# A gated linear attention with a fast-product MLP: exp(L) stored with adjacent words, single first loads, a LayerNorm step moved, and a new sequence of turns

## The chip, the cores and the metric

The kernel runs on one core of one Trainium2 chip. The metric is the device time of one execution in microseconds (us), the median of several runs. The engines are TensorE (PE; its weight loads are PEld), VectorE (DVE), ScalarE (ACT), GpSimd (POOL) and SyncE (SP), whose queue issues almost all DMAs here. [...]

## The reference

Two blocks follow each other. The first is a recurrent gated linear attention over 4 batches, 8 heads, 768 tokens and heads of 48:

```python
for t in range(S):
    state = alpha[:, :, t, :, None] * state + einsum('bhd,bhe->bhde', k[:, :, t], v[:, :, t])
    y[:, :, t] = einsum('bhd,bhde->bhe', q[:, :, t], state)
```

The second is a feed-forward block on the heads side by side (rows of 384), with the weights given as 64-bit floats:

```python
xn = (x - mean(x)) / sqrt(var(x) + 1e-06) * g_ln
out = x + maximum(xn @ w_ch1, 0.0) @ w_ch2        # 384 -> 1536 -> 384
```

## The kernel before, in words

The 768 tokens are cut into six chunks of 128. `attention(c, b)` treats chunk c of batch b, 24 units in all. With L the running sum of log(alpha) within a chunk (or within each half chunk of 64 tokens from chunk 1 on), k is divided by exp(L) and q multiplied by it, so that attention inside the chunk is a masked product of matrices and the state is carried from half to half.

A unit goes like this. ScalarE takes the logarithm of alpha (L285). TensorE sums it with a triangular matrix into PSUM (`lps`, L288). ScalarE writes exp(L) into the tile `eq` in SBUF (L291) and exp(-L) in place (L292). VectorE forms k·exp(-L) (L294) and q·exp(L) (L296) in the tile `qk`. TensorE transposes both (`tps`, L323), ScalarE or VectorE copies them out (`kT`, and `qT` or `at`; L328 to L333), TensorE multiplies them (`aps`, L340 or L345), and VectorE copies the allowed half into `at` (L353, L356). TensorE forms the update of the state (`ups`, L372), which VectorE adds to the state `st` (L384 in chunk 0, L387 later) and GpSimd multiplies by the gate (L389). TensorE forms the output (`yps`, L399). ScalarE copies it to `x` (L403). LayerNorm follows: statistics on VectorE (L418, L419), the reciprocal deviation on ScalarE (L422, L423), and the last step `xn`, which is one VectorE instruction (L427) in chunks 0 and 1, and from chunk 2 on a small VectorE instruction (L430) and one on ScalarE (L432). TensorE transposes `xn` (`xps`, L439) and ScalarE copies it to `xT` (L441).

The gate is exp(L) of the last token of the half: it lies in one row of `eq` (one partition) and is needed as a column. L301 stores that row to DRAM (`row`), L361 loads it back turned (`gate`). In `eq` the index of the head pair p runs fastest, so each exp writes words four apart, and the gate load reads four adjacent words for each partition.

The MLP works by chunk on all four batches. In chunk 0 it is plain: hidden products (L462, `hidden`), projections (L474, `project`). From chunk 1 on both products use fast schemes with fewer products: 15 for the first layer on sums of weight blocks and of token blocks (L702, `hidden_product`), 20 for the second (L545, `product`). The sums of the weights are formed once, on GpSimd (L655, the turns "S") and VectorE (L505, "W"), those of the inputs per chunk on VectorE (L678, "X"; L532, "N"). Products are combined from PSUM by VectorE and GpSimd (L710 to L745), and ScalarE applies the ReLU (L754, "R").

The weights come as 64-bit floats in twelve pieces of 768 KB (`take_weights`, turns "A" to "L"). Three staging buffers `ws` hold them; VectorE and ScalarE turn each piece into 32-bit floats (L203 to L218). A piece is loaded (L191) when an earlier one has left its buffer.

Everything is written as generators. The string `ORDER` names, one letter per step, which generator goes on: "a" to "x" are the 24 attention units (four letters per chunk), "M" the MLP, "O" the reloading of `x` for the final addition. This string sets the order of every queue:

```python
with tc.manual_schedule():
    for turn in ORDER:
        next(turns[turn], None)
```

Of the kernel before, what the change touches and what calls it, by code (L numbers as in the profile page):

```python
# [9 lines left out]
FP32 = mybir.dt.float32  # L10
# [12 lines left out]


ORDER = (
    "bbBBaddbcccaaaabbdccadabbcbbaaaabdacbbbcccbAcfcaabddddadbeBAbfffeeAgaeeaaccccdbb"
    "chbcaaaaaabbhcdddahfeefAeggghddAddcccbceefffabacefdddbdjcedccfffddDDjgeeeiMMMeeB"
    "iCCDCMMMgCiieeMeejCFMMgggBEEMfjDMfffhhEEfffjigFFfMggggHHeGMMFMGHfhMffgIGMhhgggOO"
    "OOMMMhMggiGJhhSSglMhhjMifHKlIIIMJJhhgiSfSkhMMiiKkeLLKLLhhMMfhheejkMjMeMeJfWeehgg"
    "WMMMFkhhhhhhhggfkMggiWWLgXXOXXXiiiXXSSSSllllmSXXiiiMiMMjMEjjjSSSSSjjMMMMMMMMMMXn"  # L30
    "SSljjjjOMXSMMMjjlMiijWliimWMMlmlklllllmmlMMMMkjjklkMMMMMMkMMmmiikkkkMRRkkMRRWkoM"
    "WWMMMMkknnklMWlljllmnRWRnMmMmjMMoMMMMMMMjjMMMMikiMoRRMMMRMMmmmmmkkkMMMomnnnMMNNo"
    "noWlmpmmRRRMMniWNNNMMMmmmnnnqnnOMMMlnnppNpppNiniMMMMoKMNNlnNMNMoMMoOMMjjNMMNlNMM"
    "NMMMMNMMnkkoooonokoMMMMoooMMkkllpqroXnnXXppMMXXXXMrrqpXXXMMMooXGrppppIpMMqnpMMMp"
    "MMMMMMMMMMMMqqsssRRMMMmmmMRqqMMnpMMMqqrMMMmrtqqqqMMMstsMMMsqqMMMMtMMMMMMqmRpoppM"
    "pRMRRMMMMRRMMRMMRNoooOOOMmmOMMNMqMMrptttsrNNNnMnMMrrMNNNMpMMMMrprrrKvMMrppNNvvMr"
    "rRNNuoJNqnnMMMMMqsqMsMMMMMNNNMMMorvppMMMMooMMssssssMXXsXOMMrMMrOrXXXXtttMMMXXrXX"
    "BssuuMMMMMMMMqMqqqMMMOMMMMMsMMqRMMMMrstCttRssttMMMMMMMMtttMMMMrRRuuvvxOMMMMMMquu"
    "uMMMwMMMMqqvRRRRMMMMMMMMRRMuMMMNNNNMMRRwtutwwwNNMMMNNNtvuuuuMttvttvAMMMMMNNNMMss"
    "ssrrMMMxrxutMMtNMMOMNMMMrMMNNtMMMMMtutxMMsssvvvvrOuuXXXXXXXvuuwMMMMwwwMMXXxXMMMM"  # L40
    "MXMMMMMMMMMMMvMxMMMMMMMMwwwwwvvxxuuuuuDMMvMMMMwMwOMMMMMMMMMxMMMMwRRRMMMxMMMMRRRM"
    "MxxxxxwMMRRRRMNuRvvwNNwwwxMMMvvMuNNNMMMMMMwMMMMMNMNxNNRNNNxxMMOvvMMMMMNMwMMMxxxx"
    "wMMwwxNMMxMMMMxNxvvMMXXMXMXXXXMMXXXMMMMMMMMMMMXMMMMMMMMMMMMMMMMMMMMMMMMMMMMMMMMM"
    "MMMMMMMMMMMMRRMRRRROOORRRRMMMMNNMMMNNRMMNNRMMMMMMNNNNMMMNMMMOMMNNMMMMMMNNMMMNMMM"
    "MMMMMHMM"
)


# [1 line left out]
def kernel(  # L50
# [36 lines left out]
    nc = tc.nc  # L87

    B, S, H, D = q.shape
    DM = H * D  # L90
    DF = w_ch1.shape[1]
    P = 128
    NCB = S // P
    NP = H // 2
# [6 lines left out]
    cpool = ctx.enter_context(tc.tile_pool(name="const", bufs=1))  # L101
# [11 lines left out]
    r = np.arange(P)  # L113
# [5 lines left out]
    def load(c, m, names):  # L119

        bs = range(2 * m, 2 * m + 2)
        rows = slice(c * P, (c + 1) * P)
        for n, src in (("a", alpha), ("k", k), ("q", q)):
            if n in names:
                t = raw.tile([P, 2, 2, NP, D], FP32, name=f"r{n}", tag=f"r{n}")
                nc.sync.dma_start(t.rearrange("t b i p d -> t b (i p d)"),
                                  src[bs.start:bs.stop, rows].rearrange("b t h d -> t b (h d)"))
                raws.update({(n, c, b): t[:, b - bs.start] for b in bs})
        if "v" in names:
            va = raw.tile([P, 2, 2, 2, NP, D], FP32, name="va", tag="va")  # L130
            if c == 0:
                nc.sync.dma_start(va[:, :, 0].rearrange("t b i p d -> t b (i p d)"),
                                  v[bs.start:bs.stop, rows].rearrange("b t h d -> t b (h d)"))
                raws.update({("v", c, b): (None, va[:, b - bs.start]) for b in bs})
                return


            rv = raw.tile([P, 2, NP, D], FP32, name="rv", tag="rv")
            src = v[bs.start:bs.stop, rows].rearrange("b (s t) (i p) d -> i s t b (p d)", s=2, i=2)
            for i in range(2):  # L140
                nc.sync.dma_start(rv[halves[i]].rearrange("t b p d -> t b (p d)"), src[i, i])
                for s in range(2):
                    nc.sync.dma_start(va[halves[1 - i], :, s, i].rearrange("t b p d -> t b (p d)"),
                                      src[i, s])
            for b in bs:
                raws["v", c, b] = rv[:, b - bs.start], va[:, b - bs.start]
# [18 lines left out]
    for m in range(B // 2):  # L165
        load(0, m, "a")
# [54 lines left out]
    def take_weights(i):  # L221
# [13 lines left out]

    more = cpool.tile([P, 4, NJ // 3 * DM // 2], FP32, name="more")
    shared = more.rearrange("p i m -> p (i m)")[:, :4 * NP * P]
    eqs = [cpool.tile([P, 2, 64, NP], FP32, name=f"eq{b}") for b in range(2)]
    eqs += [shared[:, i * NP * P:(i + 1) * NP * P].rearrange(
        "p (b c a) -> p b c a", b=2, c=64) for i in range(2)]  # L240
    qks = [cpool.tile([P, 2, NP, 2, 64], FP32, name=f"qk{b}") for b in range(3)]
    qks.append(shared[:, 2 * NP * P:].rearrange("p (i a b c) -> p i a b c", i=2, b=2, c=64))
    sts = [cpool.tile([R, NP, D], FP32, name=f"st{b}") for b in range(B)]
    for b in range(B):
        nc.vector.memset(eqs[b][:, :, D:], 0.0)
        nc.vector.memset(qks[b].rearrange("p i a b c -> p (i a b) c")[:, :, D:], 0.0)


# [6 lines left out]
    def eq_of(c, b):  # L255
        return eqs[b if c < 2 else b % 2]

    def qk_of(c, b):
        return qks[b if c < 2 else b % 3]
# [12 lines left out]
    def attention(c, b):  # L272


        whole, last = c == 0, c + 1 == NCB
        if whole and b % 2 == 0:
            load(0, b // 2, "kq")
            yield
            load(0, b // 2, "v")
            yield  # L280

        qk = qk_of(c, b).rearrange("t n p i c -> t n i p c")[:, :, :, :, :D]
        eq = eq_of(c, b).rearrange("t i c p -> t i p c")[:, :, :, :D]
        la = work.tile([P, 2, NP, D], FP32, name="la", tag="la")
        nc.scalar.activation(out=la, in_=raws.pop(("a", c, b)), func=AFT.Ln)  # L285
        yield
# [10 lines left out]
        ends = slice(P - 1, P) if whole else slice(HS - 1, P, HS)  # L297
        ne = 1 if whole else 2
        row = dram.tile([2, 2 * 64 * NP], FP32, name="row", tag="row")
        gate = work.tile([P, 2, NP], FP32, name="gate", tag="gate", bufs=B)  # L300
        nc.sync.dma_start(row[:ne], eq_of(c, b)[ends].rearrange("o i c p -> o (i c p)"))  # L301
        yield
        n = c * B + b + 2
        if c < 2 and b % 2:
# [14 lines left out]
        rows = [slice(0, 64), slice(64, R)]  # L319
# [28 lines left out]
        for i in range(2):  # L348
            h = slice(0, P) if whole else halves[1 - i]
# [8 lines left out]
                    mask=mask[h, h].unsqueeze(1).unsqueeze(1).broadcast_to([HS, NP, 2, HS]))  # L358
        yield
        with nc.allow_non_contiguous_dma(reason="two rows to columns"):  # L360
            nc.sync.dma_start(gate[:, :ne], row[:ne].rearrange("o (r p) -> r o p", p=NP))  # L361
        yield
        rv, va = raws.pop(("v", c, b))
        heads = [slice(0, 64), slice(64, R)]
# [58 lines left out]
        nc.scalar.activation(out=rstd[:, :1], in_=rstd[:, :1], func=AFT.Exp, scale=-0.5)  # L423
        yield
        xn = work.tile([P, DM], FP32, name="xn", tag="xn", bufs=2)
        if c < 2:
            nc.vector.tensor_scalar(out=xn, in0=x, scalar1=mv[:, 0:1], scalar2=rstd[:, :1],  # L427
                                    op0=AOP.subtract, op1=AOP.mult)
        else:
            nc.vector.scalar_tensor_tensor(out=rstd[:, 1:], in0=mv[:, 0:1], scalar=-1.0,  # L430
                                           in1=rstd[:, :1], op0=AOP.mult, op1=AOP.mult)
            nc.scalar.activation(out=xn, in_=x, func=AFT.Identity, scale=rstd[:, :1],  # L432
                                 bias=rstd[:, 1:])
# [323 lines left out]
    def mlp():  # L757
        for c in range(NCB):
# [12 lines left out]
            for n in SECOND:  # L771
                yield from product(c, n)

    turns = {chr(ord("a") + n): attention(n // B, n % B) for n in range(NCB * B)}
    turns |= {chr(ord("A") + i): take_weights(i) for i in range(len(pieces))}
    turns |= {"M": mlp(), "S": combine_first(), "W": combine_weights(), "R": relus(),
# [34 lines left out]
```

## Time and profile before

| | us |
|---|---|
| median of 3 runs (lowest, highest) | 482.97 (481.81, 483.08) |
| the profiled execution | 481.5 |
| its span on the core | 479.7 |
| TensorE busy in the span | 454.8 |
| VectorE busy | 366.5 |
| ScalarE busy | 219.8 |
| GpSimd busy | 177.6 |

The mean granted clock of TensorE was 0.989. The busy time of TensorE is modelled at the ends of its pipelined matmuls, so it overstates the work. Lines such as L427 are lines of this kernel; a group in the profile is written as engine, operation, output<-inputs, shapes and count, then busy us and mean ns of one, then the idle time of the engine just before and what ended it. The chain of waits follows the execution back from its last instruction, at each step to what released it.

### The profile page before, as it was taken

The page shows a single profiled execution, that of the slowest core. Times are in us where ns is not written, and L with a number is a line of the kernel's source. Part 1 is how long each engine was busy: PE and PEld are TensorE (multiplying, and loading weights), DVE is VectorE, ACT ScalarE, POOL GpSimd, SP SyncE. Part 2 cuts the span into 40 slices and gives each one's busy share as a digit, 9 for nine tenths or more (in the row PEclk, how much of TensorE's full clock was granted, in tenths as well). Part 3 has the DMA queues.
Part 4 walks back from the last instruction along what each step waited for, and adds up shares of the span by engine and source line. Part 5 has one row for each costly group of instructions (what it writes and reads, how often), then busy time and mean ns, then how long its engine had stood idle before and what let it go on. Part 6 is the DMA issues. An engine that isn't in the chain of part 4 may idle for free.

```text
span 479.7 us, 10173 instructions
## 1 busy us (share of the span) xinstructions
PE 454.8 (95%) x4010; PEld 377.1 (79%) x4010; DVE 366.5 (76%) x687; ACT 219.8 (46%) x463; POOL 177.6 (37%) x199
## 2 busy tenths in 40 slices
PE   6898989997999999999999999999999999998996
PEld 4676454664678889998789898889998899977896
DVE  4798999877758979958978777669767687775683
ACT  4497655534226766345556515555242733213300
POOL 1000040335088571141752242670325450434613
PEclk9899999998999999999999999999999999999999
DMA  8938578233142332222225015022112010120001
GB/s 270 316 89 267 168 248 256 89 83 122 34 129 59 102 108 68 84 67 84 83 86 165 3 50 164 20 84 64 58 40 60 1 51 1 58 91 0 1 10 57
DMA packets 41224, 45.47 MB, mean 95 GB/s; under 512 B 9773, under 2 KB 37293, under 8 KB 41177
## 3 DMA queue, kind: packets, MB, share of 16 engines
q1 hardware_dynamic: 40632, 44.69, 30.0%
q8 instruction: 31, 0.51, 0.4%
q10 hardware_dynamic: 544, 0.13, 0.2%
q14 instruction: 17, 0.13, 0.1%
HBM read 35.28 MB, written 9.53 MB: 93 GB/s over the span
## 4 chain that ended last, share of the span: by engine, by line
PE 54%; DVE 23%; POOL 8%; DMA 5%; ACT 5%; issue 4%; SPq 0%; POOLq 0%; DVEq 0%; ACTq 0%
PE ops L545 20%; PE hps L702 18%; DMA ws<-in_moe_w_ch_dram 5%; PE ops L474 3%; PE aps L345 3%; PE yps L399 2%; PE tps L323 2%; DVE w L205 2%; PE lps L288 2%; DVE at L356 2%; DVE sum L678 2%; DVE qk L296 2%; DVE ws L211 2%; DVE sum L532 2%; PE ups L372 1%
## 5 line engine op out<-in xcount | busy, mean ns | idle before, releaser
L389 POOL TENSOR_TENSOR st<-st,gate 112x192 f32<-112x192 f32 x36 | 27.3, 762 | 129.1 <-DVE st L387 99.8
L702 PE MATMUL hps<-sum,w 128*128 128x256 f32 x240 | 59.1, 381 | 1.1 <-DVE hT L745 1.1
L561 POOL TENSOR_TENSOR ob<-ob,u 128x192 f32<-128x192 f32 x40 | 25.5, 647 | 73.7 <-DVE ob L558 52.0
L702 PEld LDWEIGHTS hps<-sum,w 128*128 128x128 f32 x240 | 44.8, 190 | 8.2 <-DVE hT L745 1.9
L545 PE MATMUL ops<-w,hT 128*128 128x192 f32 x280 | 50.1, 328 | 0.0
L545 PEld LDWEIGHTS ops<-w,hT 128*128 128x128 f32 x280 | 45.6, 190 | 0.7 <-DVE ob L555 0.2
L754 ACT ACTIVATE hT<-hT 128x512 f32<-128x512 f32 x60 | 34.3, 622 | 15.3 <-POOL hT L740 5.1
L379 ACT COPY va<-st 64x192 f32<-64x192 f32 x80 | 27.9, 348 | 27.3 <-POOL st L389 26.5
L356 DVE COPY_PREDICATED at<-consts,aps 64x512 f32<-64x512 int32 x40 | 29.2, 731 | 10.7 <-PE aps L345 9.5
L462 PE MATMUL hps<-xT,w 128*128 128x512 f32 x72 | 33.5, 612 | 0.6 <-ACT x L403 0.6
L474 PE MATMUL ops<-w,hT 128*128 128x384 f32 x96 | 33.3, 500 | 0.0
L399 PEld LDWEIGHTS yps<-va,at 128*64 128x64 f32 (+1 forms) x768 | 24.9, 137 | 10.5 <-issue 5.6
L702 PE MATMUL hps<-xT,w 128*128 128x256 f32 x120 | 31.7, 387 | 1.1 <-DVE hT L734 1.0
L399 PE MATMUL yps<-va,at 128*64 128x48 f32 (+1 forms) x768 | 28.3, 224 | 2.7 <-ACT va L379 2.4
L721 POOL TENSOR_TENSOR hT<-hT,u 128x512 f32<-128x512 f32 x10 | 12.8, 1283 | 48.0 <-DVE u L720 48.0
L545 PE MATMUL ops<-ws,hT 128*128 128x192 f32 x160 | 29.6, 328 | 0.1
L545 PE MATMUL ops<-ws,sum 128*128 128x192 f32 x160 | 29.1, 328 | 0.2 <-DVE ob L558 0.2
L323 PE MATMUL tps<-consts,qk 128*112 128x128 f32 x176 | 26.9, 283 | 1.8 <-DVE qk L294 1.2
L333 ACT COPY at<-tps 64x512 f32<-64x512 f32 (+1 forms) x40 | 23.1, 578 | 11.5 <-PE tps L323 7.5
L474 PEld LDWEIGHTS ops<-w,hT 128*128 128x128 f32 x96 | 18.5, 198 | 11.9 <-issue 0.9
L545 PEld LDWEIGHTS ops<-ws,sum 128*128 128x128 f32 x160 | 26.2, 190 | 0.9 <-DVE ob L558 0.5
L323 PEld LDWEIGHTS tps<-consts,qk 128*112 128x112 f32 x176 | 20.4, 137 | 8.1 <-DVE qk L294 2.1
(154 smaller groups left out, 1051.3 us busy)
## 6 DMA issues: line engine op xcount, KB each, us to landing
ws<-in_moe_w_ch_dram SPq DMA_DIRECT2D x12, 768.0 KB
kept<-x SPq DMA_DIRECT2D x24, 192.0 KB
ob<-kept SPq DMA_DIRECT2D x24, 192.0 KB
va<-in_v_dram SPq DMA_DIRECT2D x40, 96.0 KB
out_dram<-ob SPq DMA_DIRECT2D x19, 192.0 KB
ra<-in_alpha_dram SPq DMA_DIRECT2D x6, 384.0 KB
rk<-in_k_dram SPq DMA_DIRECT2D x6, 384.0 KB
rq<-in_q_dram SPq DMA_DIRECT2D x6, 384.0 KB
```

Of the source, the lines that this page charges most:

```text
L323: nc.tensor.transpose(tps[:, p], qk_of(c, b)[:, i, p].rearrange("p a b -> p (a b)")[:, :R], ident)
L333: nc.scalar.copy(out=at[rows[j], :, j], in_=tv[rows[j]])
L356: nc.vector.copy_predicated(out=at[h, :, i], data=aps[i][h], mask=mask[h, h].unsqueeze(1).unsqueeze(1).broadcast_to([HS, NP, 2, HS]))
L379: nc.scalar.copy(out=to[h, s, i], in_=st[h])
L389: nc.gpsimd.tensor_mul(st, st, by)
L399: nc.tensor.matmul(yps[halves[s], i, p], at[rs, p, i, s], va[rs, 0 if whole else s, i, p], start=True, stop=True)
L462: nc.tensor.matmul(hps, w1[:, f, j * P:(j + 1) * P], xT_of[c][:, f], start=(f == 0), stop=(f == NF - 1))
L474: nc.tensor.matmul(ops_of[b], hT_of[c][:, j, b], w2[:, j], start=(j == 0), stop=(j == NJ - 1))
L545: nc.tensor.matmul(acc, lhs[:, j], rhs[:, j], start=(j == 0), stop=(j == NT - 1))
L561: getattr(nc.gpsimd, f"tensor_{op}")(x, x, y)
L702: nc.tensor.matmul(acc[:, i], w, b, start=True, stop=True)
L754: nc.scalar.activation(out=x, in_=x, func=AFT.Relu)
```

## The change

Four things change. The tile `eq` gets the layout [pair, half, word], so that each exp writes, and each product reads, runs of adjacent words; the row stored to DRAM keeps this order, and the gate load reads single words 128 apart. The alphas of chunk 0 are loaded with one DMA per batch instead of one per two batches. LayerNorm's last step goes to ScalarE from chunk 1 on instead of from chunk 2 on (`whole` is true in chunk 0 only). And `ORDER` is another string with the same letters in the same numbers; only its beginning is shown.

```diff
 ORDER = (
-    "bbBBaddbcccaaaabbdccadabbcbbaaaabdacbbbcccbAcfcaabddddadbeBAbfffeeAgaeeaaccccdbb"
-    "chbcaaaaaabbhcdddahfeefAeggghddAddcccbceefffabacefdddbdjcedccfffddDDjgeeeiMMMeeB"
+    "aBaaabaaabbbbacccadaaaddBbbbdcbbdcceaaaaccbbbbABBfddcabccdddeeceabfgAffaaAccecch"
+    "cbbeggdfgbccacbbbdddbfeedeeddfgaaeaafeeeeCddedcffhafeddcceecOfBeaegbbgfccecdddhg"
...
@@ load @@
-                nc.sync.dma_start(t.rearrange("t b i p d -> t b (i p d)"),
-                                  src[bs.start:bs.stop, rows].rearrange("b t h d -> t b (h d)"))
+                step = 1 if n == "a" and c == 0 else 2
+                for i in range(0, 2, step):
+                    nc.sync.dma_start(
+                        t[:, i:i + step].rearrange("t b i p d -> t b (i p d)"),
+                        src[bs.start + i:bs.start + i + step, rows].rearrange(
+                            "b t h d -> t b (h d)"))
...
-    eqs = [cpool.tile([P, 2, 64, NP], FP32, name=f"eq{b}") for b in range(2)]
+    eqs = [cpool.tile([P, NP, 2, 64], FP32, name=f"eq{b}") for b in range(2)]
     eqs += [shared[:, i * NP * P:(i + 1) * NP * P].rearrange(
-        "p (b c a) -> p b c a", b=2, c=64) for i in range(2)]
+        "p (a b c) -> p a b c", b=2, c=64) for i in range(2)]
...
-        nc.vector.memset(eqs[b][:, :, D:], 0.0)
+        nc.vector.memset(eqs[b].rearrange("p a b c -> p (a b) c")[:, :, D:], 0.0)
...
@@ attention @@
-        eq = eq_of(c, b).rearrange("t i c p -> t i p c")[:, :, :, :D]
+        eq = eq_of(c, b).rearrange("t p i c -> t i p c")[:, :, :, :D]
...
-        nc.sync.dma_start(row[:ne], eq_of(c, b)[ends].rearrange("o i c p -> o (i c p)"))
+        nc.sync.dma_start(row[:ne], eq_of(c, b)[ends].rearrange("o p i c -> o (p i c)"))
...
-            nc.sync.dma_start(gate[:, :ne], row[:ne].rearrange("o (r p) -> r o p", p=NP))
+            nc.sync.dma_start(gate[:, :ne], row[:ne].rearrange("o (p r) -> r o p", p=NP))
...
-        if c < 2:
+        if whole:
             nc.vector.tensor_scalar(out=xn, in0=x, scalar1=mv[:, 0:1], scalar2=rstd[:, :1],
                                     op0=AOP.subtract, op1=AOP.mult)
```

Lines of the changed kernel stand four further down from the alphas' load on.

More of the change, by code (lines that the diff above doesn't have):

```diff
@@ L25 @@
 ORDER = (
-    "bbBBaddbcccaaaabbdccadabbcbbaaaabdacbbbcccbAcfcaabddddadbeBAbfffeeAgaeeaaccccdbb"
-    "chbcaaaaaabbhcdddahfeefAeggghddAddcccbceefffabacefdddbdjcedccfffddDDjgeeeiMMMeeB"
[L28 to L43, printed above, removed]
@@ L44 @@
-    "MMMMMMMMMMMMRRMRRRROOORRRRMMMMNNMMMNNRMMNNRMMMMMMNNNNMMMNMMMOMMNNMMMMMMNNMMMNMMM"
-    "MMMMMHMM"
+    "aBaaabaaabbbbacccadaaaddBbbbdcbbdcceaaaaccbbbbABBfddcabccdddeeceabfgAffaaAccecch"
+    "cbbeggdfgbccacbbbdddbfeedeeddfgaaeaafeeeeCddedcffhafeddcceecOfBeaegbbgfccecdddhg"
+    "gAAfMMfCECfffCCgfMhhiMMMEMMiiEfDjhFkDDiiFFfggMMMhghMMMMffkDGGkEEHHhhGgkFjgjHMijj"
+    "GggMMSMgggggSJhhJjkhhhhHffMMMJfefMMIiiKIiiIIMMOOhhhhhOihhggLLiliiLhKKWeeMMklkllW"
+    "WWIeejjiiliMMMMMSiSSSSSggelfhhhejgMfMhjWgghXXXMXjjjjXSSXXjSXXXiMnjjMMninjMjnjiWl"
@@ new lines @@
+    "llSlnmWiMMMMMMMXSSMMSSMMMMSkMMMjjiiOOkkOWiMMMmMmlllljjjMMMMnMMMMMMMMRjpkkMMGMMMM"
+    "llmMMMWmmWolRRMMMMllllMWnRRnknOiRkkknMMiMMMRMMMMkkkkRMkpRMiimmmmMMjMMMjjHNNmmWmm"
+    "MMMMRRMRNmmNMMmmNNNNMnnnlnnMppMMMpooopnnnMMMMorroqnnnmmNNNroNMMkllkkMMMNNMMMlMMk"
+    "noWkoolMMNNMMkMqMMmlllMppMMkkrXXXXXXXMMMXXoommmooMMMoMMpopoorMrMMppppMppXXMMMMMt"
+    "toqpqtMMMrppmmRMMMMmqMqsMMMRMMRoprMMnnnpqqMMMMooMMMMMMppMpoooMMqMMMMMqqOOOOqqqtM"
+    "MMMMMqqMRRRRRRMMMMsRMMssnoopprmJmtMMMMRNNtNNvrMRoMtqMqrrronrNMssuMMrMBNNMpMvDNMM"
@@ new lines @@
+    "MMNNrNMnnMMrrMMNNMrMppNNMvMMvNMMMMMMMMMAqOXXXXXXrrqqsMMMMsssXXXXXMMMMMMOMKrrMMqt"
+    "ttMMMMMMrssssssMuuMMMMsssMMMMMqqttttMMtqMMRRMRuuutttMMMMMMqsrrrwtvtttqCMMvMMMMMv"
+    "vsuuMMMsMMRRvwstuuvMMMMwssMMMMMvvvvvvwMMwwRuuRuuuqRROORNNMNMRMMNNMMMMMMMNMMttNNN"
+    "MMMMMtrMRtNNNMMMrMMqssMMNNMNNMMMMMtMMMMxxxxMMssMtXXXXXXXXXXxMMvvuuuwwwXMMMMMMMMM"
+    "uuuuxMMMMMMMxMMMMMMRROxMMwvMMMMvxMMMMwvwwwRRMRMMMMwMMxwMMMMMuMMMxxxxuuxMMMMMMMMM"
+    "MRRMMRRRxxMMMOMMOMNNRMNwNNNxNwMMMMMMwwwNNNRxxMMMMxNMMOMMMNNMMMwwvMMvvvxxxMMwMMux"
@@ L46 @@
+    "NNNMMMMuxwxMMwwMvvXXXXXXXMXMMMMMMXXXMMMMMMMMMMMMMMMMMMMMMRRRMMMRLLMMMOKMMMMMMMMM"
+    "MMMMMMMMMMMRRRRMMMMMMMMRRJOOOFMMMMNNNNMRRMMMMMNNNNMMMMMMMNNNMMMMMMNNMMMMMMMNNMMM"
+    "MNMMMMMM"
 )
```

## The prediction

> **What bounds the kernel now.** I read the page first: busy shares, then the span in 40 slices.
>
> ```profile
> PE 454.8 (95%) x4010; PEld 377.1 (79%) x4010; DVE 366.5 (76%) x687; ACT 219.8 (46%) x463; POOL 177.6 (37%) x199
> ...
> PE   6898989997999999999999999999999999998996
> ...
> DVE  4798999877758979958978777669767687775683
> ```
>
> From slice 10 (120 us) on TensorE is full and VectorE is not; before that VectorE is the full one. To see what each stage costs, I add up the work that stands ahead of a step in TensorE's own queue, and subtract the sum from the time at which the step starts: I call this the lag. The sums take the order of the program's instructions and the spacing of matmul records in back-to-back runs (chain of waits: 48 records of L702 in 10.36 us, 128 of L545 in 21.17, 8 of L474 in 2.58; a matmul is two records, a transpose one). Before: first hidden product (L462) 29.6 us of work ahead, starts at 45.8, lag 16.2; first projection (L474) 72.9, 92.9, lag 20.0; fifth projection group 88.6, 108.5, lag 19.9; sixth 92.1, 115.6, lag 23.5; first product of chunk 1 (L702) 113.1, 136.8, lag 23.7; the same line in the last chunk 395.5, 421.4, lag 25.9; near the end 441.3, 470.6, lag 29.3. So 23.7 of the 29.3 us that TensorE loses are lost before 137 us, 3.5 of them between the fifth and the sixth group. The chain of waits, in order of time, shows those:
>
> ```profile
> 110.83 4.02 DVE xn L427
> 114.85 0.04 issue
> 114.89 0.90 PE xps L439 x3
> 115.79 6.21 PE ops L474 x16
> ```
>
> and the timeline shows why a step that takes 0.48 us elsewhere took 4.01:
>
> ```profile
> 110.49 4.12 POOL L655 TENSOR_TENSOR w<-w 128x384 f32<-128x384 f32 x6
> ...
> 110.83 4.01 DVE L427 TENSOR_SCALAR xn<-x,mv,rstd 128x384 f32<-128x384 f32 x1 [1.56 <-ACT rstd L423]
> ```
>
> It ran exactly until GpSimd's row of six ended. From 24 to 107 us the chain is mostly VectorE rounding weights, with DMA waits. VectorE's own lag moves little there: L211 of the second weight piece has 26.8 us ahead and starts at 35.1 (8.3); the last L214 ends with 94.5 done, at 106.8 (12.3).
>
> [...] the exp that writes every fourth word (L291) takes 879 ns, the same exp in place (L292) 606; the product that reads it (L296) takes at least 840, its twin without a stride (L294) 544. [...] In the packet records the 16-byte packets of a gate load start 5.8 ns apart within a burst, far below the loads' 1536-byte packets (median 65 ns each).
>
> ```profile
> L291 ACT ACTIVATE eq<-lps 128x384 f32<-128x384 f32 x20 | 17.6, 879 | 10.4 <-PE hps L702 5.6 <-PE lps L288 4.6
> L292 ACT ACTIVATE lps<-lps 128x384 f32<-128x384 f32 x24 | 14.5, 606 | 0.0
> ...
> L432 ACT ACTIVATE xn<-x,rstd 128x384 f32<-128x384 f32 x16 | 11.3, 707 | 33.7 <-DVE rstd L430 33.7
> ```
>
> ```profile
> L296 DVE TENSOR_TENSOR qk<-rq,eq 128x384 f32<-128x384 f32 x20 | 19.0, 955 | 0.0
> ```
>
> **The change part by part.** *exp(L) with adjacent words.* 24 exps lose 0.27 us of latency each on ScalarE (the next instruction starts 0.65 after such an exp, 0.51 to 0.57 after L292, so occupancy falls less, some 2.5 us in all). 24 products lose 0.28 to 0.30 each (0.84 to about 0.55): 7 us. Only those in VectorE's full stage count: 11 stand ahead of the last weight piece in the new order, 3.2 us.
>
> *The gate load* (L361) now gathers single words: 512 or 1024 packets for 128 or 256, 22,528 instead of 5,632. Lower bound by the bursts: 16 engines, 8 or 16 packets each before, 32 or 64 after, at 5.8 ns: 0.14 or 0.28 us later per load. Upper bound: the two loads under heavy traffic spread over 2.16 and 3.06 us; if that spread were the packets' own cost and not the engines' unequal backlogs, it would quadruple, 6.5 to 9.2 us more. Within them each engine's eight packets come in one burst of 41 ns, so I take the lower one. Behind a late gate stand L384 in VectorE's queue and SP's queue, whose DMAs reuse eight semaphores.
>
> *First alphas singly:* two more issues on SP, 0.48 us each, and the first weight piece after them. TensorE's warm-up matmuls run until 6.7 us anyway and the first Ln starts at 4.8, so I cost this at 0; bounds -0.5 and +1.
>
> *LayerNorm of chunk 1:* four L427 leave VectorE (0.48 each, one of 4.01), four L430 come (0.13 to 0.84, mean 0.27) and four L432 on ScalarE (0.71 each, 2.8 us). ScalarE was 9.8 of 23.1 us busy from 93 to 116, so it has room. The stall of 3.5 us goes unless L430, which reads SBUF twice, waits as long; its worst of sixteen took 0.84.
>
> *The new sequence.* The listing of both programs' queues shows what moves. When the last weight piece is rounded, VectorE has 94.5 us done before and 94.7 after, but the new queue holds one more pair of L294 and L296, two more L356 and one more L387 by then: TensorE stands at 81.8 instead of 79.3. At its first L702 TensorE has 117.6 us done instead of 113.1, with VectorE at 115.5 and 115.2. What TensorE has to wait for is the position of the producer in VectorE's queue less its own position, plus VectorE's lag. The largest differences before: 7.6 (fourth xn of chunk 0), 8.0 (third piece of w1), 8.7 (w2, middle third); 7.6 and 8.0 plus VectorE's 8.9 us give 16.5 and 16.9 where TensorE's lag was 16.6 and 17.0, so the measure holds. After, they are 5.6 (first piece), 5.5 (third and fourth, and `at`), 6.1 (w2, last third).
>
> VectorE's lag after: it starts on the first batch's products at about 9.3 us instead of rounding a piece at 9.0, equal. A weight piece loads when an earlier one's buffer is free and SP's queue has come to it. Before, issue to use took 4.4 to 6.9 us. In the new order only the tenth has its buffer freed too late (4.3 us of VectorE work ahead of its use, so about 1 us of wait). The seventh to ninth stand behind six value loads for chunk 2, which wait for L399 at 44.2 us of TensorE work, about 60 us on the clock; six issues take 3.7, so the seventh is issued near 64.5 and lands near 69.5, and VectorE comes to it at 61.4 + 8.9 = 70.3. Close, but in time. So VectorE ends the weights with a lag of 9 to 12.3; I take 10.5. TensorE's lag is then 6.1 + 10.5 = 16.6, plus 0.9 for small waits (before it ran up to 1.2 above the measure): 17.5 at the first L702. GpSimd's sums of w1 in the new order start after an L389 near 111 us and need 20.3 us to the first operand of L702: 131.3 - 117.6 = 13.7, no bound.
>
> *Sum.* 23.7 - 17.5 = 6.2 us less: 3.5 from the vanished stall, 2.7 from VectorE's queue. After that both kernels are full of TensorE work. Before loses 5.6 more us, 3.4 of them in the last chunk, where GpSimd's seven additions of 1.28 per half (9.0 us) exceed TensorE's 15 products (6.5); this stays. So the profiled execution goes from its 481.5 us (span 479.7, 1.8 around it) to 475.3. It was 1.5 below the median of the runs, 482.97; that median less 6.2 gives 476.8, rounded to 477.0.
>
> **The rivals.** *A: the weight loads come late.* For: the seventh piece has 0.8 us to spare, and all three then load at once. Against: their buffers are free long before. Each us of lateness idles VectorE and comes back as lag at w2's last third; at 6 us nothing is gained: 480 to 483. *B: the gate loads become slow (slower than before).* At the upper bound the second gate lands 9.2 us later; before it had 2.8 us until its L384, so VectorE stands for 6.4 us, then again for the third and fourth gates, unloaded before (0.39 and 0.46 us spread), +1.2 each with 1 us to spare. With 6.4 + 0.4 against 6.2 the kernel ends 0.6 later; with waits of SP behind it (one DMA in eight reuses the semaphore) 2 to 4 more: 484 to 487. It decides once the first two gates take 6 us longer together with the slack. *C: new waits in the main stage.* After 137 us before loses only 2.2 us up to the last chunk; a sequence that meets its waits less well could lose 3 to 6 more: 480 to 483. Against it: in both orders no attention matmul follows its producer's matmul closer than the steps between take.
>
> **How the numbers follow.** Main case 0.64; A 0.16, half of it still faster; B 0.07; C 0.13, about a third still faster. About 0.3% (1.4 us) is what a measurement of this kernel can tell from no change. Faster 0.64 + 0.08 + 0.05 = 0.77; within 0.3% 0.10 out of A and C; slower 0.13, B and the rest. The range: low, the lag can't fall below 5.6 + 8.9 = 14.5 (9.2 us gained), with 1.3 more from the main stage: 472.5. High, A or C without any gain: 483.0; most of B lies outside.
>
> **What would show it.** Right: L291 near 0.61 and L296 near 0.55; four more L432 and no L427 after 50 us; TensorE at its first L702 near 135 us with no wait over 1 us before L439; waits of VectorE for `ws` no longer than before. Wrong: VectorE idle before L384 (gates), or before L203 by more than 5 us in 65 to 90 us (A); lag growing after 137 us (C); a long L430 while GpSimd adds weights.

## The result and the profile after

| us | before | after |
|---|---|---|
| median of 18 runs each | 482.16 (479.38 to 483.25) | 479.4 (475.69 to 482.82) |
| the profiled execution | 481.5 | 477.88 |
| its span | 479.7 | 476.1 |
| mean granted clock | 0.989 | 0.988 |

The ratio of the times is 0.9942, 95% interval [0.9921, 0.9963]: faster by 0.58%, or 2.8 us. The forecast was 477.0 us, 6.2 us less. The direction held, the size was about half. How so much got lost is the subject of what follows.

The page of the changed kernel, with the rows of TensorE, VectorE and TensorE's granted clock over 40 slices of 11.9 us:

```profile
span 476.1 us, 10196 instructions
...
PE 450.6 (95%) x4010; PEld 374.6 (79%) x4010; DVE 364.8 (77%) x687; ACT 214.3 (45%) x467; POOL 172.8 (36%) x199
...
PE   6899979998698999999999999999999999988996
...
DVE  3988989998589868868678876868866677765683
...
PEclk9999989999799999999999999999999999999999
```

From slice 2 on TensorE shows 9 in most slices. Its deepest hole after the start is slice 10, 119 to 131 us, with 6 where before shows 9, and the granted clock is down to 7 there. That hole is new; before's stall at L427 lies in its slice 9, which shows 7.

The lag of the prediction (the time at which a step of TensorE starts, less the sum of the work ahead of it in its queue), at the same steps in both traces:

| step | before: starts, lag | after: starts, lag |
|---|---|---|
| first hidden product of chunk 0 | 45.8, 16.2 | 43.3, 11.2 |
| sixth projection group | 108.5, 19.9 | 106.1, 14.8 |
| ninth group | 122.2, 24.4 | 114.9, 14.5 |
| eleventh group | 129.4, 24.0 | 129.9, 21.4 |
| first product of chunk 1 | 136.8, 23.6 | 138.8, 21.3 |
| seventh product | 142.5, 23.6 | 145.8, 23.0 |
| near the end | 474.5, 29.2 | 470.8, 25.6 |

(Counted anew, the groups that the prediction calls fifth and sixth, at 108.5 and 115.6 us, are the sixth and seventh of twelve.) By the ninth group the changed kernel was 9.9 us better, more than the 6.2 forecast. Then, up to the eleventh, it lost 6.9 us. The chain of waits names the place, in order of time (start, us, what):

```profile
112.51 9.01 DVE rstd L434 x2
121.53 0.01 issue
121.54 0.07 ACT xn L436
121.61 0.67 issue
122.28 0.48 ACT xT L445
122.75 0.61 ACT xn L436
123.36 0.38 ACT xT L445
123.74 0.04 issue
123.78 0.90 PE xps L443 x3
124.68 1.92 PE ops L478 x3
```

L434 of the changed kernel is L430 of the one before, the instruction that forms -mean*rstd, one element per partition. All its executions in the changed kernel (min, median and longest ns, first and last start):

```profile
L434 DVE SCALAR_TENSOR_TENSOR rstd<-mv,rstd x20: 129/150/8933, 88.9 to 411.5; 128x1 f32<-128x1 f32 x20
```

The same view of the kernel before:

```profile
L430 DVE SCALAR_TENSOR_TENSOR rstd<-mv,rstd x16: 133/154/843, 171.9 to 413.2; 128x1 f32<-128x1 f32 x16
```

One took 8.93 us where the median is 0.15. The timeline of GpSimd in the changed kernel shows what ran beside it; the idle time before an instruction stands in brackets, and only the first and the last lines of an uninterrupted row of weight sums (L659) are copied:

```profile
107.93 0.75 POOL L393 TENSOR_TENSOR st<-st,gate 112x192 f32<-112x192 f32 x1 [11.77 <-DVE st L391]
108.64 1.00 POOL L659 TENSOR_TENSOR ra<-ra,w 128x384 f32<-128x384 f32 x1
...
119.57 1.40 POOL L659 TENSOR_TENSOR w<-w 128x384 f32<-128x384 f32 x2
120.92 0.51 POOL L393 TENSOR_TENSOR st<-st,gate 112x192 f32<-112x192 f32 x1
```

The row ends at 121.43 and L434 at 121.4. It is the picture of L427 in the kernel before, with a longer row and another instruction in the trap.

TensorE's wait is not the whole of the 6.9 us: it lasted 5.2 (117.6 to 122.8). From 120.0 to 126.9 us the trace shows a granted clock of 0.50, and the eight records of the tenth group took 3.9 us instead of 2.6, so some 1.3 us were lost after the wait. The kernel before has 0.50 from 114.4 to 117.8 us, at the end of its own stall.

A second stall follows, again from the chain of waits:

```profile
137.49 5.33 DVE w L509
142.82 0.07 DVE qk L300
142.89 0.33 issue
143.21 0.94 DVE w L509
144.15 0.61 DVE hT L716
144.76 0.04 issue
144.81 1.42 PE hps L706 x5
```

L509, a sum of two weight blocks in SBUF that takes 0.95 us otherwise, stood behind GpSimd's next row (it adds weights from 135.08 to 142.0), and the VectorE addition that a hidden product hangs on stood behind L509: 1.7 us more of lag.

The groups of the changed kernel that answer to L292, L296 and L291 (busy us, mean ns of one, idle before):

```profile
L296 ACT ACTIVATE lps<-lps 128x384 f32<-128x384 f32 x24 | 11.8, 493 | 0.0
L300 DVE TENSOR_TENSOR qk<-rq,eq 128x384 f32<-128x384 f32 x20 | 11.1, 554 | 0.0
L295 ACT ACTIVATE eq<-lps 128x384 f32<-128x384 f32 x20 | 9.8, 492 | 21.0 <-PE lps L292 21.0
```

The first exp fell from 879 to 492 ns, the product from 955 to 554, and the second exp, whose layout did not change, from 606 to 493.

### The profile page after: what moved, and what is told of

Read it like the earlier page. It is cut to its first block, busy times and chain, and to the rows that moved or that the text cites. A ratio compares the mean times of both kernels' runs of the same rounds, so it can differ in the third digit from the quotient of the medians.

```text
span 476.1 us, 10196 instructions
## 1 busy us (share of the span) xinstructions
PE 450.6 (95%) x4010; PEld 374.6 (79%) x4010; DVE 364.8 (77%) x687; ACT 214.3 (45%) x467; POOL 172.8 (36%) x199
## 4 chain that ended last, share of the span: by engine, by line
PE 61%; DVE 16%; DMA 7%; POOL 5%; issue 4%; ACT 2%; SPq 1%; POOLq 0%; DVEq 0%; ACTq 0%
PE ops L549 24%; PE hps L706 22%; DMA ws<-in_moe_w_ch_dram 5%; PE yps L403 3%; PE aps L349 2%; DVE sum L682 2%; PE tps L327 2%; PE lps L292 2%; DVE rstd L434 2%; PE ops L478 2%; PE ups L376 2%; DVE w L209 1%; DVE w L509 1%; DVE ws L215 1%; DMA ra<-in_alpha_dram 1%
## 5 line engine op out<-in xcount | busy, mean ns | idle before, releaser
L393 POOL TENSOR_TENSOR st<-st,gate 112x192 f32<-112x192 f32 x36 | 20.8, 580 | 126.5 <-DVE st L391 106.2
L565 POOL TENSOR_TENSOR ob<-ob,u 128x192 f32<-128x192 f32 x40 | 28.4, 721 | 80.4 <-DVE ob L562 57.5
L758 ACT ACTIVATE hT<-hT 128x512 f32<-128x512 f32 x60 | 35.6, 626 | 26.5 <-POOL hT L728 11.6
L403 PEld LDWEIGHTS yps<-va,at 128*64 128x64 f32 (+1 forms) x768 | 23.7, 137 | 6.2 <-issue 4.7
L478 PEld LDWEIGHTS ops<-w,hT 128*128 128x128 f32 x96 | 18.5, 198 | 11.8 <-issue 1.1
L559 DVE TENSOR_TENSOR ob<-ops,ob 128x192 f32<-128x192 f32 x50 | 17.4, 352 | 13.5 <-PE ops L549 6.0
L327 PE MATMUL tps<-consts,qk 128*112 128x128 f32 x176 | 25.3, 275 | 2.0 <-DVE qk L300 1.5
L466 PEld LDWEIGHTS hps<-xT,w 128*128 128x128 f32 x72 | 13.9, 198 | 16.4 <-issue 15.2
L549 PEld LDWEIGHTS ops<-ws,hT 128*128 128x128 f32 x160 | 26.3, 190 | 0.6
L436 ACT ACTIVATE xn<-x,rstd 128x384 f32<-128x384 f32 x20 | 14.2, 710 | 27.5 <-DVE rstd L434 25.5
```

The costliest lines, as they stand in the source:

```text
L327: nc.tensor.transpose(tps[:, p], qk_of(c, b)[:, i, p].rearrange("p a b -> p (a b)")[:, :R], ident)
L393: nc.gpsimd.tensor_mul(st, st, by)
L403: nc.tensor.matmul(yps[halves[s], i, p], at[rs, p, i, s], va[rs, 0 if whole else s, i, p], start=True, stop=True)
L466: nc.tensor.matmul(hps, w1[:, f, j * P:(j + 1) * P], xT_of[c][:, f], start=(f == 0), stop=(f == NF - 1))
L478: nc.tensor.matmul(ops_of[b], hT_of[c][:, j, b], w2[:, j], start=(j == 0), stop=(j == NJ - 1))
L549: nc.tensor.matmul(acc, lhs[:, j], rhs[:, j], start=(j == 0), stop=(j == NT - 1))
```

## The experiments

Twelve kernels ran. "Lag" is the lag at the first product of chunk 1. The ratios, with 95% intervals, are to executions of the kernel before that ran beside each set (its medians there: 482.1 to 482.7); they differ by up to 0.3% from the quotients of the medians shown, and carry the comparisons.

| kernel | sequence | exp layout and alphas | LayerNorm of chunk 1 | lag | us | ratio |
|---|---|---|---|---|---|---|
| before | old | old | VectorE, whole | 23.6 | 482.2 | 1 |
| after | new | new | L434 | 21.3 | 479.4 | 0.9942 [0.9921, 0.9963] |
| e1 | new | new | all ScalarE | 14.9 | 471.7 | 0.9804 [0.9774, 0.9833] |
| e2 | new | new | VectorE, whole | 19.6 | 477.75 | 0.9921 [0.9893, 0.995] |
| e3 | old | new | L434 | 21.4 | 476.9 | 0.9913 [0.9873, 0.9953] |
| e4 | new | old | VectorE, whole | 23.3 | 480.8 | 0.9992 [0.9972, 1.0012] |
| f1 | old | new | all ScalarE | 20.9 | 476.5 | 0.9874 [0.9824, 0.9923] |
| f2 | new | old exp | all ScalarE | 14.1 | 472.8 | 0.9792 [0.976, 0.9824] |
| f3 | new | old alphas | all ScalarE | 15.2 | 470.9 | 0.976 [0.9716, 0.9803] |
| f4 | old | old | all ScalarE | 22.8 | 480.2 | 0.9947 [0.9917, 0.9978] |
| g1 | old, W later | new | all ScalarE | 14.4 | 471.7 | 0.9801 [0.977, 0.9832] |
| g2 | new | old | all ScalarE | 14.0 | 472.8 | 0.9821 [0.9792, 0.9851] |
| g3 | old, W later | old | all ScalarE | 19.1 | 476.6 | 0.9912 [0.9884, 0.994] |
| g4 | old | old | L430 | 25.5 | 483.4 | 1.0033 [1.0014, 1.0053] |

**Is L434 the loss? (e1)** The changed kernel, but -mean*rstd comes from two small activations on ScalarE:

```diff
-            nc.vector.scalar_tensor_tensor(out=rstd[:, 1:], in0=mv[:, 0:1], scalar=-1.0,
-                                           in1=rstd[:, :1], op0=AOP.mult, op1=AOP.mult)
+            nc.scalar.activation(out=rstd[:, 1:], in_=mv[:, 0:1], func=AFT.Identity,
+                                 scale=rstd[:, :1])
+            nc.scalar.activation(out=rstd[:, 1:], in_=rstd[:, 1:], func=AFT.Identity, scale=-1.0)
```

> The changed kernel, but from chunk 1 on -mean*rstd is formed by two small activations on ScalarE instead of VectorE's L434. Theory (a new stall at L434: [...] the stall moved from L427 to L434 and grew to 8.9 us, which costs TensorE about 6 us): L443 of that batch starts near 113.5 instead of 123.8 us, the weight sum of W that is next in VectorE's queue [...] takes the wait in its place, until GpSimd's row ends at about 121, but nothing of TensorE's hangs on it at once; TensorE's lag at its first product of chunk 1 falls from 21.3 to 15 to 17, and the time is 4 to 6 us under the changed kernel's, 473.5 to 475.5. Rival 1 (the stall only passes to the next instruction of VectorE's queue, and the sums of xT behind it come no earlier): 479, no change against the changed kernel. Rival 2 (the missing gain is elsewhere: gates, weight loads, main stage): no more than 1 us under the changed kernel.

471.7 us, 7.7 less than the changed kernel, more than was expected: the lag at the first product of chunk 1 is 14.9, 6.4 less, TensorE has neither the wait at this place nor the stretch at half clock, and the later stall of L509 shrank (two sums of W and the L300 between them took 5.3 us there instead of 6.7). VectorE's timeline shows that the wait did not vanish:

```profile
111.89 0.53 DVE L422 BATCH_NORM_STATS2 stats<-x 128x6 f32<-128x384 f32 x1
112.46 0.18 DVE L423 BATCH_NORM_AGGREGATE mv<-stats 128x2 f32<-128x6 f32 x1
112.56 11.15 DVE L510 TENSOR_TENSOR ws<-ws,w 128x768 f32<-128x768 f32 x1
123.63 0.75 DVE L683 TENSOR_TENSOR sum<-xT 128x256 f32<-128x256 f32 x2
```

The next instruction with two SBUF operands, a sum of W, now takes 11.15 us: it waits for GpSimd's row, which starts at 110.05 and ends here, with an L393 of 0.50, at 122.89. But all four batches' statistics are behind VectorE by then, so ScalarE and TensorE go on with LayerNorm, and TensorE has projections enough until the sums of xT come. The first two statistics lines also show what does not wait: bn_stats, with one SBUF operand, takes its usual 0.5 us in the middle of the row. So the stall at L434 is the loss, and both rivals fall.

**Would the old form have waited less? (e2)** The changed kernel with chunk 1's LayerNorm back on VectorE:

```diff
-        if whole:
+        if c < 2:
             nc.vector.tensor_scalar(out=xn, in0=x, scalar1=mv[:, 0:1], scalar2=rstd[:, :1],
```

> The changed kernel with the LayerNorm of chunk 1 back on VectorE (one tensor_scalar of 128x384 as before), the new sequence and all else kept. Theory (whichever of the two forms stands there waits for the end of GpSimd's row): the tensor_scalar of the batch that comes first takes about 8 to 9.5 us, the time is within 1.5 us of the changed kernel's, 478.5 to 481. Rival (the tiny instruction with two SBUF inputs is the culprit, and the tensor_scalar, which reads SBUF once, would wait less, as its 4.0 us before): 475 to 477, 3 us or more under the changed kernel.

All executions of that line in this kernel (min, median and longest ns):

```profile
L431 DVE TENSOR_SCALAR xn<-x,mv,rstd x8: 452/473/9835, 32.8 to 121.7; 128x384 f32<-128x384 f32 x8
```

9.8 us against 8.9: the tensor_scalar is caught in the same row. The time, 477.75, is a little under the 478.5 of the theory and not under the changed kernel's beyond the intervals. The rival (475 to 477) is out. Moving the last step as the change does bought nothing.

**The sequence without the parts, and the parts without the sequence (e3, e4).** e3 is the changed kernel with the old ORDER, e4 the kernel before with the new one; no other line differs. The edit of e3, of which e4 is the reverse on the other kernel (first line of the string only):

```diff
 ORDER = (
-    "aBaaabaaabbbbacccadaaaddBbbbdcbbdcceaaaaccbbbbABBfddcabccdddeeceabfgAffaaAccecch"
+    "bbBBaddbcccaaaabbdccadabbcbbaaaabdacbbbcccbAcfcaabddddadbeBAbfffeeAgaeeaaccccdbb"
...
```

> The changed kernel's three code parts (exp layout, single alphas, LayerNorm on ScalarE from chunk 1) with the sequence of turns of the kernel before. Theory (the sequence gave the 4 to 5 us of lag gained before 88 us; the code parts only shorten VectorE's queue by 11 products of 0.29 us, and L434 waits for GpSimd's row of six as L427 did): L434 of the sixth group takes 3 to 4 us, lag at the first product of chunk 1 21 to 23 against 23.7, the time 0.5 to 2.5 us under before's, 479.5 to 481.5. Rival (the parts give the gain and the sequence nothing): 478.5 to 479.5, as the changed kernel. Rival (single-word gates cost): above before's 482.

> The kernel before with the new sequence of turns alone (exp(L) strided, alphas in pairs, LayerNorm of chunks 0 and 1 on VectorE). Theory: the sequence lets VectorE's producers stand 2.4 us earlier but the strided exps and products keep 3.2 us in VectorE's full stage, and LayerNorm's tensor_scalar waits 8 to 9 us behind GpSimd's longer row of sums; so the time is 480.5 to 483, at most 1.5 us under before's. Rival (the sequence gives it all, the parts nothing): 478.5 to 479.5.

e3 took 476.9, 2.6 us under the lower end of the theory and as good as the changed kernel within the intervals; e4 cannot be told from the kernel before. My view that the sequence made the early gain was wrong, at least in this form: at the fifth group e3 has a lag of 15.1 with the old sequence, e4 16.7, after 14.8, before 19.9. Either one gives 3 to 5 us there, and both together hardly more. And each has its stall: one L434 of 3.67 us in e3, one L427 of 9.8 us in e4.

**Parts and sequence without L434 (f1, f2, f3).** e1 with the old ORDER (f1), with the strided exp and 16-byte gate packets (f2), with the first alphas in pairs (f3). f1 has the ORDER of e3; the edits of f2 (tile, exp and gate load; the zeroing, the shared tiles and the stored row follow) and of f3:

```diff
-    eqs = [cpool.tile([P, NP, 2, 64], FP32, name=f"eq{b}") for b in range(2)]
+    eqs = [cpool.tile([P, 2, 64, NP], FP32, name=f"eq{b}") for b in range(2)]
...
-        eq = eq_of(c, b).rearrange("t p i c -> t i p c")[:, :, :, :D]
+        eq = eq_of(c, b).rearrange("t i c p -> t i p c")[:, :, :, :D]
...
-            nc.sync.dma_start(gate[:, :ne], row[:ne].rearrange("o (p r) -> r o p", p=NP))
+            nc.sync.dma_start(gate[:, :ne], row[:ne].rearrange("o (r p) -> r o p", p=NP))
```

```diff
-                step = 1 if n == "a" and c == 0 else 2
+                step = 2
```

> The three code parts with -mean*rstd on ScalarE (the version that took 471.7 us), but with the sequence of turns of the kernel before. Theory 1 (the three code parts give the whole gain, the new sequence none of it): no stall behind GpSimd's row of six either, lag at the first product of chunk 1 near 16, 471 to 473.5. Theory 2 (the sequence is worth some 3 us, which its longer GpSimd row of sums took back as long as L434 stood on VectorE): 474 to 476.5.

> The version with -mean*rstd on ScalarE (471.7 us), new sequence, but exp(L) stored with the four pairs interleaved as before (and its gate load in 16-byte packets again). Theory 1 (the layout is worth the 11 products of 0.29 us that stand in VectorE's full stage, and on top of that the exps and products of the first batches, which stand on the way to the first hidden product): 3.5 to 5.5 us slower, 475 to 477. Theory 2 (the slack of TensorE hides most of it): under 2 us, 472 to 473.5. If single-word gate packets cost something hidden so far, the loss would be smaller than 3 us as well, with VectorE's queue as late as in theory 1.

> The version with -mean*rstd on ScalarE (471.7 us), new sequence, but the first alphas loaded in pairs of batches again. Prediction's term (0, between -0.5 and +1): 471 to 472.5. Rival (the first Ln waits for its alphas, so the first exps, products and weight pieces come later one for one): first L289 about 1 us later, 472.5 to 473.5.

f1 took 476.5, in theory 2's range, so the sequence seemed to be worth 3 to 5 us. f2 took 472.8, in theory 2's range: in the new sequence the layout of exp(L) brings nothing that the intervals could show. f3, at 470.9, says the same of the alphas (prediction's term: 0). The traces show a part of why. At the first hidden product e1 stands at a lag of 11.8, f2 at 13.4, f3 at 15.7. At the seventh (66 to 68 us) they stand at 15.9, 14.7 and 16.9: the lead is gone by the time half of the weight pieces are rounded.

**Why does the old sequence lose with LayerNorm on ScalarE? (f4, then g1 and g3)** f4 is the kernel before with e1's LayerNorm from chunk 1 on: e1's diff, and

```diff
-        if c < 2:
+        if whole:
```

> The kernel before with its LayerNorm's last step on ScalarE from chunk 1 on and -mean*rstd formed there as well; nothing else changed. The prediction's term for that (the stall of 3.5 us goes): no L427 after chunk 0, L439 of that batch about 3.5 us earlier, lag at the first product of chunk 1 20 to 20.5 against 23.7, 478 to 479.5. Rival (the two-input instruction behind it in VectorE's queue takes over the wait and TensorE hangs on it just as much): 481 to 482.5.

480.2, between the two: 2.5 us less than the 482.7 of the kernel before beside it, but the lag fell by 0.8 only, and the profiled spans differ by 1.3. VectorE's timeline of f1, which has the same sequence, shows the place:

```profile
106.87 7.32 DVE L510 TENSOR_TENSOR ws<-w 128x768 f32<-128x768 f32 x2
114.11 0.55 DVE L483 TENSOR_TENSOR ob<-ops,ob 128x384 f32<-128x384 f32 x1
114.58 0.54 DVE L298 TENSOR_TENSOR qk<-rk,lps 128x384 f32<-128x384 f32 x1
115.04 0.55 DVE L422 BATCH_NORM_STATS2 stats<-x 128x6 f32<-128x384 f32 x1
```

The sum of W again takes over the wait, but in the old sequence the statistics of the next batch (L422) are queued behind it, and TensorE waits for that batch's transposes. If so, moving the two turns of W behind them must help. The stretch of ORDER concerned, as one string, in g1 (f1 with it) and g3 (f4 with it):

```diff
-    "MjMeMeJfWeehggWMMMFkhhhhhhhggfkMggiWWLg"
+    "MjMeMeJfeehggMMMFkhhhhhhhggfkMggiWWWWLg"
```

> Old sequence of turns, the three code parts, -mean*rstd on ScalarE (476.5 us without the edit of this run), and now the two turns of W that stand ahead of the statistics of the batches h and g moved behind their LayerNorm. Theory (with L434 gone, the wait for GpSimd's row went over to the first of those W sums, 7.3 us for two, and in the old sequence the next batch's statistics stand behind it in VectorE's queue, so TensorE still waits at L444; in the new sequence all four batches' statistics stand ahead of it): the wait moves behind the statistics, lag at the first product of chunk 1 falls from 20.9 to 16 to 17.5, 471.5 to 473.5. Rival (the old sequence is slower for other reasons): 475.5 to 477.

> The kernel before with LayerNorm's last step and -mean*rstd on ScalarE from chunk 1 on, and the two turns of W moved behind the LayerNorm of the batches h and g; exp layout, alphas and the rest of the sequence as before. Theory (the term of 3.5 us in the prediction is there, once nothing with two SBUF operands stands ahead of the LayerNorm in VectorE's queue): lag at the first product of chunk 1 about 20 instead of 22.8 with the old place of W, 477 to 479. Rival: 480, as without moving W.

g1 took 471.7, as fast as e1, and g3 476.6, by the medians 3.6 under f4 (the intervals of the two ratios overlap) and 5.9 under the 482.5 of the kernel before beside it. Both lags came where the theory put them or lower (14.4, 19.1). In g1's timeline of VectorE the statistics run before the sums, and the four sums come when GpSimd's row is over:

```profile
108.52 0.53 DVE L422 BATCH_NORM_STATS2 stats<-x 128x6 f32<-128x384 f32 x1
109.15 0.18 DVE L423 BATCH_NORM_AGGREGATE mv<-stats 128x2 f32<-128x6 f32 x1
109.25 1.59 DVE L300 TENSOR_TENSOR qk<-rq,eq 128x384 f32<-128x384 f32 x1
110.76 3.55 DVE L510 TENSOR_TENSOR ws<-w 128x768 f32<-128x768 f32 x4
```

So the old sequence was not slower for other reasons.

**Part 3 as the change makes it, alone (g4), and the new sequence with ScalarE's LayerNorm alone (g2).** g4 is the kernel before with f4's last diff alone (-mean*rstd stays L430). g2 is f2 with f3's edit.

> The kernel before with LayerNorm's last step on ScalarE from chunk 1 on as the change does it (-mean*rstd on VectorE, L430), and nothing else. Prediction's term: L430 takes at most about 1 us, 3.5 us less, 478 to 479.5. Theory now (L430 waits for GpSimd's row of six as L427 did): one L430 of 3.5 to 4 us, no change, 481 to 483.

> New sequence and LayerNorm's last step with -mean*rstd on ScalarE, but exp(L) strided and the first alphas in pairs, both as before. Theory (what these two parts give by 44 us is lost again by 70 us, where the weight pieces and alphas come from DMA at about the same time in every version with the new sequence): 471.5 to 473.5, within 1.5 us of the version with all parts (471.7). Rival (each was hidden behind the other; without both VectorE's full stage is 3 to 5 us longer): 475 to 477.

g4 is slower than the kernel before, 1.0033 [1.0014, 1.0053]: the step that the prediction put at -3.5 us. Its chain of waits, in order of time:

```profile
111.39 3.29 DVE rstd L430
114.68 0.02 issue
114.70 0.72 ACT xn L432
115.42 0.04 issue
115.46 0.90 PE xps L439 x3
```

L430 waits 3.29 us for the row that L427 waited for, and then ScalarE needs 0.72 us where VectorE needed 0.48. The granted clock was 0.50 for 6.8 us from 114.1, in that wait and after it, where before has 3.4 us of it. The theory's range was 481 to 483, with an L430 of 3.5 to 4 us. g2 took 472.8, as its theory said.

The four versions without a stall on TensorE's path make a square: old sequence with W later, 476.6 without the layout and the alphas and 471.7 with them (g3, g1); new sequence, 472.8 without and 471.7 with (g2, e1). The lag at the first product says the same: 19.1 with neither, 14.0 with the sequence, 14.4 with layout and alphas, 14.9 with both. Each takes about 5 us off, and the second to come finds nothing left. The five fastest versions, e1, f2, f3, g1 and g2, are not told apart by their intervals; each takes about 2% off the time before.

## Why the prediction was right in direction and wrong in size

*The failing step: "The stall of 3.5 us goes unless L430, which reads SBUF twice, waits as long; its worst of sixteen took 0.84."* It waits as long, and longer: 8.93 us in the changed kernel, 3.28 where part 3 stands alone (g4). The prediction named "a long L430 while GpSimd adds weights" as what would prove it wrong, and then took the sixteen executions of the kernel before as evidence against it. They lay after 171.9 us, where GpSimd runs no weight sums (its last one in that kernel starts at 144.7); they could not tell. The 3.5 us were also too low a price for a stall: the half clock at its end (0.50 for 3.4 us from 114.4) belongs to it, and before's lag went from 19.9 at the sixth group to 24.4 at the ninth. In the changed kernel one element per partition was enough for the wait (L434, 128x1), while a bn_stats of 128x384 took its usual 0.53 us in the same row. And the wait was not for one GpSimd instruction, of 0.46 or 1.00 us, but until a whole row of back-to-back ones was over (13 of after's 18 sums and an L393). Why VectorE waits, the traces do not show. Not every row held it so long, as the last section shows.

*GpSimd's sums, "no bound".* For the operand of the first product that held: no TensorE wait was for them. But the row was costed only for who needs its results, and not for whom it locks out. In the new sequence VectorE reaches LayerNorm of batch h at 112.5 us with 9 us of row left; in the old one L427 came with 4 us left.

*VectorE's queue: 2.7 us, from a lag of 10.5 at the last weight piece.* Too small. VectorE ended the weights at 102.8 us with 94.7 done, a lag of 8.1; with the measured 6.1 of the new sequence that makes 14.2, and TensorE stood at 14.5 at the ninth group. VectorE's waits for weights were 2.9 us in three, the longest 1.9, where before had 11.0 in five, 6.2 of it at the start. The lag after the first piece was expected to grow and did not. The measure itself (VectorE's lag plus the largest distance to a producer) held a second time.

*The stage after 137 us, costed at 0.* Before loses 5.6 us from the first product of chunk 1 to the end, after 4.3, and that with 1.7 for L509. So 3.0 were gained there and 1.7 lost, rival C in a small way. From the seventh product to the end the seven kernels with adjacent exps lose 2.2 to 3.4 us, the seven with strided ones 4.8 to 6.2, with either sequence and with granted clocks of 0.985 to 0.998 in both lots: the layout is worth something there too, though TensorE is full. Which waits of TensorE it shortens is open. In the new sequence without the stall little of it is left at the end: f2, with strided exps, stands 1.7 us ahead of e1 at the seventh product (lags of 14.2 and 15.9) and 1.2 behind it near the end. The prediction put before's loss in the last chunk down to GpSimd, whose additions of 9.0 us a half exceed 15 products of 6.5. That sum took two records for each product, where the trace has four: 60 records of 0.216 us are 12.9, so GpSimd is not the longer one, and the trace puts TensorE's waits there (3.1 us in the kernel before) to VectorE.

*The sum.* Span before less span after is 3.6: 9.1 gained (a lag of 14.5 at the ninth group against the 23.6 of before's first product), 6.9 lost at L434 (5.2 in the wait, some 1.3 at half clock behind it) with 0.1 won back by the first product, 1.7 lost at L509, 3.0 gained later. The medians differ by 2.8, and either one lies far from 6.2. That the time fell within the range was luck: a gain that was underestimated met a loss that was not seen.

*What held.* Exp and product: 0.61 and 0.55 expected, 0.49 and 0.55 measured. The gate load: 16,928 packets more, and no VectorE idle time before L388, where rival B had put 6.4 us; the lower bound was the right end. GpSimd's L393 did wait for a gate twice (released at 48.6 and 220.2 us), but so it does in f2, with packets of 16 bytes. The alphas at 0: f3. The weight loads: rival A did not come. Its near relation did: what exps and alphas win by 44 us is gone by 70 us in every version with the new sequence. That DMA arrivals (weights and the alphas of chunk 1) set that floor fits the chain of waits of the changed kernel, which there holds loads of `ws` and `ra` of 4.6 to 8.2 us, but no run took them away, so it stays open. Open, too, is why layout and alphas are worth 3.4 us in the new sequence with its stall (e2 against e4, 0.9921 against 0.9992) and about 1 without it; in the profiled executions the half clock behind the stall lasts 3.4 us in e2 and 6.8 in e4, which explains at most half of it.

## What to carry to other kernels

When an instruction stalls until another engine's row of work is over (L427, 4.01 us), ask which other instructions would wait there before moving the work: here the wait went on to the next instruction of the same kind in the queue (8.93 us at L434, and 11.15 at a sum of W once -mean*rstd was on ScalarE), and what counts is what is queued behind that one. Cost a row of GpSimd instructions twice: for the engines that wait for its results and, as the worst case, for VectorE's two-operand instructions, which in the rows of these stalls came in only at the end. Put work that ran through such a row at its usual length (bn_stats, 0.53 us; L391 with one operand in PSUM, 0.36), and everything that TensorE hangs on, ahead of the first of them. An instruction's mean from a stage without the disturber says nothing of its cost beside it (L430 of the kernel before: 0.27 us in the mean; the same instruction as L434 of the changed kernel: 8.93 in the row).

## What the runs showed of the hardware that I had not expected

In the rows of weight sums that made the stalls above, a VectorE instruction with two SBUF operands, or the tensor_scalar of 128x384, came in only when the row was over: 8.93 us for 128x1 (else 0.15), 9.84 for the tensor_scalar (else 0.47), 11.15 for a sum of 128x768 (else 0.95), each ending within about an instruction's length of the row's end. GpSimd's own instructions keep their 1.00 and 0.46 us meanwhile. bn_stats (0.53 us) and the addition with one operand in PSUM (L391, 0.36) run through the same rows at their usual length.

Not every row does this. The next row of e1 let VectorE in several times, and there it was GpSimd that waited (a sum of 128x128 takes 0.46 us otherwise):

```profile
130.89 1.00 POOL L660 TENSOR_TENSOR rq<-rq,rk 128x384 f32<-128x384 f32 x1
131.20 1.51 DVE L510 TENSOR_TENSOR w<-w 128x768 f32<-128x768 f32 x1
131.85 1.18 POOL L660 TENSOR_TENSOR extra<-extra 128x128 f32<-128x128 f32 x1
132.63 1.77 DVE L300 TENSOR_TENSOR qk<-rq,eq 128x384 f32<-128x384 f32 x1
```

In these traces the instructions that got in had mostly come while the first or second GpSimd instruction after a pause, or after VectorE's last turn, was running (L510 above came in the second, L393 being the first), and those that waited to the end had come later (L427 of the kernel before in the sixth, L434 of the changed kernel in the seventh). There are exceptions: L203 of the kernel before, at 100.7 us, came in the fourth of five and went ahead of the fifth (it took 0.61 us, and the fifth, a sum of 128x128, 0.77). No run varied this, so what decides is open.

A wait of TensorE costs more than its length here: behind the 5.2 us of the changed kernel, eight records took 3.9 us instead of 2.6. In the seven profiles (before, after, e2, e3, e4, f1, g4) in which TensorE waited 3.0 to 5.4 us at once between 100 and 130 us, a stretch of 3.4 or 6.8 us with a granted clock of 0.5 begins during that wait; in the other seven, whose longest wait there is 1.6 us, none does.

The exp in place in PSUM (L292, 606 ns) became 493 ns when the exp ahead of it wrote adjacent words: the strided writes had cost the instruction behind them as well. With strided exps its mean is 606 ns in before, 604 in e4, 600 in f2, 603 in g2 and 605 in g4; with adjacent ones 493 in after, 489 in e1 and 494 in f1.
